# Three score steps in one row-tiled visit: a static order rebuilt on a refitted model

## The chip, the cores and the metric

The kernel runs on one core of a Trainium2 chip. The metric is the device time of one execution in microseconds. The kernel before takes 408.64 us in the median of 3 runs (407.82 to 408.83).

## The reference

Input is one sequence of 2048 tokens with 512 features in bf16. The same pair of blocks is applied twice, with the same weights.

```python
def _A_ref(x, wqkv, wo):              # H = 32 heads of 16, window W = 256
    qkv = (x @ wqkv).reshape(B, S, 3, H, Dh).transpose(2, 0, 3, 1, 4)
    scores = jnp.einsum("bhqd,bhkd->bhqk", q, k) * (Dh ** -0.5)
    mask = (idx[:, None] - idx[None, :] >= 0) & (idx[:, None] - idx[None, :] < W)
    p = _softmax(jnp.where(mask[None, None], scores, -1e9))
    o = jnp.einsum("bhqk,bhkd->bhqd", p, v)
    return o.transpose(0, 2, 1, 3).reshape(B, S, D) @ wo
def _B_ref(x, w_r, w_gate, w_up, w_down):
    r = x @ w_r
    ...                               # the ONE token with the largest r
    y = (_silu(x_sel @ w_gate) * (x_sel @ w_up)) @ w_down * _sigmoid(r_sel)
    return x + upd                    # y added to that token's row
x = x + _A_ref(_layernorm(x), A_wqkv, A_wo)
x = x + _B_ref(_layernorm(x), B_w_r, B_w_gate, B_w_up, B_w_down)
```

So each layer is attention over a sliding window of 256 keys for every token, and a gated MLP of width 1792 for a single token, which can be named only when all tokens of the layer have been through attention.

## The kernel before, in words

The 2048 tokens are cut into 16 tiles of 128 in each layer, 32 in all. For one tile the work runs like this (PE is TensorE, DVE VectorE, ACT ScalarE, POOL GpSimd, SP the queue of SyncE):

- *Layer norm:* statistics on DVE (L699, L700), the rest on POOL, and a transpose by DMA into XNT (L715).
- *Projections:* q and k with 16 matmuls each, V with 4 wide ones. DVE evacuates each: V at L768, q at L1050, k at L753. From k, four more DVE instructions (L756) write four copies, each masked to one of four groups of heads, so that one matmul can serve four heads. All three projections and the output projection take turns in one PSUM bank, number 7.
- *Scores:* nine steps in a steady tile (4 and 8 in the first two tiles of a layer). A step is a function `scores` on PE, 8 to 16 matmuls that use half the rows of the array each (64*128, "row-tiled"); it writes one pair of the six score banks, pairs taken in turn (`b0 = 2 * (n % 3)`). One ACT instruction (L1182) takes the exponential of the pair. POOL masks the windows' edges in four places of a tile (L1188).
- *PV:* 96 matmuls of 128x68 on the full array (L1212) collect values and row sums in bank 6, in two halves of 48. After each half DVE takes a reciprocal (L781) and normalises (L783).
- *Output:* the normalised tile is transposed by DMA into OT, the output projection follows (4 wide matmuls, L796), and DVE adds the residual (L800). Then come the router's dot product and the statistics for the next layer.

Between the layers the router's maximum is found, the MLP of the one token runs on PE (L875 to L970), and DVE adds the row (`upd`, L981); at the end the same again.

Nothing of this order is decided on the chip. While the program is built, a class `Sched` collects every operation with its engine, what it reads and writes, a duration in ns and a priority, and plays a list scheduler: the free engine takes, of the operations that are ready, the one with the smallest priority number. What comes out is one fixed instruction list for each engine, with semaphore waits where one needs another's result. So a duration or a priority changes only the order of the lists. Priorities are counted in tiles: `ln`, `prj`, `attend` and `fin` put a tile's layer norm, projections, attention and output at `(n - 2.4)`, `(n - 0.8)`, `n` and `(n + 1.3)` tile times.

`bind` ties steps together. Where PE changes between row-tiled and full-array matmuls, the array has to be emptied; steps that are tied run as one *visit* to the row-tiled mode. Before, each odd step is tied to the even one ahead of it:

```python
if n % 2:
    S.bind(self.tied, i)
self.tied = i
```

`cut` marks the place of the branch after the first MLP: operations that start in the model's time before `upd` ends plus 200 ns stand ahead of it in each engine's list, the others behind.

Of the kernel before, what the change touches and what calls it, by code (L numbers as in the profile page):

```python
# [57 lines left out]
class _Op:  # L58
    __slots__ = ("idx", "eng", "fn", "deps", "dur", "name", "is_dma", "prio", "signals", "count",
                 "dma_sem", "start", "end", "waits", "dma_extra", "soft", "tr", "keys", "layer", "glue")  # L60

    def __init__(self, idx, eng, fn, deps, dur, name, is_dma, prio):
# [19 lines left out]
        self.glue = None  # L82


class Sched:
    ENGS = ("pe", "act", "dve", "pool", "sp")

# [79 lines left out]
    def bind(self, i, j):  # L167
        a, b = self.ops[i], self.ops[j]
        a.glue = j
        for d in b.deps:  # L170
            if d != i:
                a.deps.add(d)
                if d in b.soft:
                    a.soft.add(d)
        b.deps.add(i)
        b.soft.add(i)

    def schedule(self):
        ops = self.ops
        n = len(ops)  # L180
# [4 lines left out]
        remaining = [len(op.deps) for op in ops]  # L185
# [31 lines left out]
        while done < n:  # L217
            best = None
            for e in self.ENGS:
# [1350 lines left out]
```

## Time and profile before

| | |
|---|---|
| median of 3 runs | 408.64 us (407.82 to 408.83) |
| profiled execution | 409.7 us |
| span of its instructions | 407.9 us |
| mean granted clock of PE | 0.946 of full |
| busy: PE, DVE, ACT, POOL | 347.8, 278.6, 266.3, 254.5 us |

Busy time counts an instruction from start to end; matmuls are pipelined, so a busy PE is not one at its peak. The span's share says which engine does much, not which one the end waits for; for that the chain of waits and the timeline of a single stretch are read.

### The profile page before, as it was taken

To read this page: it belongs to the slowest core of one execution; us is meant where nothing else is said; L and a number is where in the kernel's file an instruction comes from. 1 tells how busy PE (TensorE), PEld (TensorE's weight loads), DVE (VectorE), ACT (ScalarE), POOL (GpSimd) and SP (SyncE) were. 2 spreads that over 40 slices of the span, in tenths; PEclk is the share of its full clock that TensorE was granted. 3 is DMA by queue.
4 is the path that set the end of the run, shared out by engine and by line. 5 is a ranking of instruction groups with operands and counts; after the bars stand their busy time and mean duration, and the time that the engine had idled before them with its cause. 6 is when DMAs were issued, how large, how long until landed. Compare 5 with 4: busy or idle time off the path is not lost.

```text
span 407.9 us, 17608 instructions
## 1 busy us (share of the span) xinstructions
PE 347.8 (85%) x7740; PEld 277.1 (68%) x7793; DVE 278.6 (68%) x695; ACT 266.3 (65%) x284; POOL 254.5 (62%) x475
## 2 busy tenths in 40 slices
PE   6689698999999998986878699798889898986970
PEld 2477586877778787775767267677777787775560
DVE  5967876877777776675674388787777676673620
ACT  1078376787878787875764078687778787878000
POOL 5768866887878686766533069887566565556300
PEclk9779799999999999999999689999999999999965
DMA  8534434444435662433221013232422335221000
GB/s 267 170 73 55 100 116 81 128 131 100 117 76 107 78 118 65 102 71 81 57 41 40 3 44 84 55 69 55 75 57 63 70 68 69 56 56 27 14 18 5
DMA packets 72723, 31.23 MB, mean 77 GB/s; under 512 B 52672, under 2 KB 72000, under 8 KB 72640
## 3 DMA queue, kind: packets, MB, share of 16 engines
q1 hardware_dynamic: 70384, 27.81, 31.9%
q10 hardware_dynamic: 2256, 2.23, 1.7%
q8 instruction: 62, 1.02, 1.2%
q14 instruction: 21, 0.17, 0.2%
HBM read 14.29 MB, written 7.87 MB: 54 GB/s over the span
## 4 chain that ended last, share of the span: by engine, by line
PE 54%; DVE 24%; ACT 8%; DMA 5%; POOL 3%; issue 3%; SPq 1%; DVEq 0%; ACTq 0%; POOLq 0%
PE f_PS L1212 18%; PE f_PS L1172 10%; PE f_PS L739 10%; DVE f_KT L756 8%; ACT f_PT L1182 8%; PE f_PS L796 6%; DVE f_KTN L753 3%; DVE f_QT L1050 2%; DVE f_JUNK L813 2%; DMA f_OT<-f_ONORM 2%; PE f_PS L765 2%; PE f_PS L1233 2%; DVE f_xres L800 2%; DVE f_ST L811 2%; PE f_PS L933 2%
## 5 line engine op out<-in xcount | busy, mean ns | idle before, releaser
L1182 ACT ACTIVATE f_PT<-f_PS 128x1024 bf16<-128x1024 f32 x276 | 263.1, 1027 | 106.9 <-PE f_PS L1172 74.8
L1188 POOL TENSOR_TENSOR f_PT<-f_PT,f_TM 128x384 bf16<-128x384 bf16 x128 | 119.6, 935 | 72.8 <-ACT f_PT L1182 71.7
L1212 PE MATMUL f_PS<-f_VBD,f_PT 128*128 128x68 bf16 x2880 | 120.1, 198 | 7.4 <-DVE f_ONORM L783 2.6
L1212 PEld LDWEIGHTS f_PS<-f_VBD,f_PT 128*128 128x128 bf16 x2880 | 106.1, 99 | 25.1 <-issue 7.1
L1172 PE MATMUL f_PS<-f_QT,f_KT 64*128 64x128 bf16 (+3 forms) x2976 | 93.8, 204 | 7.1 <-DVE f_QT L1050 3.1
L1172 PEld LDWEIGHTS f_PS<-f_QT,f_KT 64*128 64x128 bf16 x2976 | 70.4, 94 | 28.3 <-ACT f_PT L1182 13.0
L739 PE MATMUL f_PS<-f_XNT,f_wqkv 128*128 128x128 bf16 x1024 | 70.5, 224 | 4.6 <-DVE f_KTN L753 1.6
L739 PEld LDWEIGHTS f_PS<-f_XNT,f_wqkv 128*128 128x128 bf16 x1024 | 60.1, 100 | 9.0 <-DVE f_KTN L753 1.8
L756 DVE TENSOR_SCALAR f_KT<-f_KTN,f_KM 128x512 bf16<-128x512 bf16 x128 | 58.5, 515 | 0.9
L796 PE MATMUL f_PS<-f_wo,f_OT 128*128 128x512 bf16 x98 | 27.9, 396 | 18.3 <-DVE f_RDA L781 9.5
L753 DVE CAST f_KTN<-f_PS 128x512 bf16<-128x512 f32 x32 | 22.1, 689 | 28.0 <-PE f_PS L739 27.9
L765 PE MATMUL f_PS<-f_wqkv,f_XNT 128*128 128x512 bf16 x108 | 29.7, 387 | 2.0 <-issue 0.9
L781 DVE RECIPROCAL f_RDA<-f_PS 128x16 f32<-128x16 f32 x64 | 16.1, 252 | 19.6 <-PE f_PS L1212 19.3
L783 DVE TENSOR_TENSOR f_ONORM<-f_PS,f_RDA 128x256 bf16<-128x256 f32 x64 | 26.5, 415 | 1.1
L768 DVE CAST f_VN<-f_PS 128x512 bf16<-128x512 f32 x32 | 22.0, 689 | 7.7 <-PE f_PS L765 7.5
L796 PEld LDWEIGHTS f_PS<-f_wo,f_OT 128*128 128x128 bf16 x128 | 10.4, 99 | 24.3 <-issue 13.7
L1170 PE MATMUL f_PS<-f_BM,f_II 64*128 64x64 bf16 (+1 forms) x256 | 24.8, 190 | 0.0
L813 DVE SCALAR_TENSOR_TENSOR f_JUNK<-f_xres,f_WR 128x512 bf16<-128x512 f32 x32 | 23.8, 743 | 0.0
L1050 DVE CAST f_QT<-f_PS 128x512 bf16<-128x512 f32 x32 | 21.8, 681 | 2.4 <-PE f_PS L739 2.4
L701 POOL TENSOR_SCALAR f_MV<-f_MV 128x1 f32<-128x1 f32 x32 | 6.1, 190 | 26.0 <-DVE f_MV L700 23.8
L811 DVE BATCH_NORM_STATS2 f_ST<-f_xres 128x6 f32<-128x512 f32 x32 | 21.5, 672 | 0.4
L800 DVE TENSOR_TENSOR f_xres<-f_PS,f_xin 128x512 f32<-128x512 f32 x16 | 11.1, 692 | 14.6 <-PE f_PS L796 14.5
(128 smaller groups left out, 306.8 us busy)
## 6 DMA issues: line engine op xcount, KB each, us to landing
f_vscr<-f_VN SPq DMA_DIRECT2D x32, 136.0 KB, 2.6
f_VBD<-f_vscr SPq DMA_DIRECT2D x128, 34.0 KB, 2.3
out_dram<-f_OUTB SPq DMA_DIRECT2D x16, 128.0 KB, 2.2
f_xin<-in_B_w_down_dram SPq DMA_DIRECT2D x14, 128.0 KB, 2.9
f_wg<-in_B_w_gate_dram SPq DMA_DIRECT2D x7, 256.0 KB, 3.7
f_wu<-in_B_w_up_dram SPq DMA_DIRECT2D x7, 256.0 KB, 3.5
f_wqkv<-in_A_wqkv_dram ACTq DMA_DIRECT2D x3, 512.0 KB, 5.6
f_xscr<-f_xres SPq DMA_DIRECT2D x5, 256.0 KB, 2.8
```

The lines of the kernel that those rows point to most:

```text
L739: r = e.matmul(self.bank(MB)[:, 128 * s:128 * s + 128], lhsT=self.wqkv[:, kc, off:off + 128], rhs=self.XNT[:, k2, kc, :], start=(kc == 0), ...
L753: S.add("dve", lambda e: e.tensor_copy(out=self.KTN[:, k2], in_=self.bank(MB)[:, 0:512].rearrange("p (s t) -> p s t", s=4)), reads=[], wri ...
L756: S.add("dve", lambda e, hh=hh: e.tensor_scalar(out=self.KT[:, k4, :, :, hh, :].rearrange("p s b k -> p (s b) k"), in0=self.KTN[:, k2].rea ...
L765: return e.matmul(self.bank(MB)[:, 0:512], lhsT=self.XNT[:, k2, kc, :], rhs=self.wqkv[:, kc, 1024:1536], start=(kc == 0), stop=(kc == 3))
L796: return e.matmul(self.bank(MB)[:, 0:512], lhsT=self.OT[:, ko, kc, :], rhs=self.wo[:, kc, :], start=(kc == 0), stop=(kc == 3))
L811: S.add(D, lambda e: e.bn_stats(out=self.ST6[:, 1, km, :], in_=x), reads=[xk], writes=["st6m%d" % km], dur=700, name="bnst2")
L813: S.add(D, lambda e: e.scalar_tensor_tensor(out=self.JUNK[:], in0=x, scalar=1.0, in1=self.WR16[:], op0=ALU.mult, op1=ALU.mult, accum_out=s ...
L1050: self.S.add("dve", lambda e: e.tensor_copy(out=self.QT[:, k2], in_=self.bank(MB)[:, 0:512].rearrange("p (s t) -> p s t", s=4)), reads=[], ...
L1172: r = e.matmul(o, lhsT=self.KT[p, (b // 4) % 4, s, b % 4].rearrange("p h k -> p (h k)"), rhs=self.QT[p, k2, s, q:q + w], start=(i == 0), s ...
L1182: S.add("act", lambda e: e.activation(out=view, in_=self.PS[:, b0:b0 + 2, 0:128 * nu].rearrange("p h (u c) -> p h u c", u=nu), func=ACTF.E ...
L1188: S.add("pool", lambda e: e.tensor_tensor(out=w, in0=w, in1=self.TM[:].unsqueeze(1).broadcast_to([128, k, 2, 32]), op=ALU.mult), reads=["t ...
L1212: r = e.matmul(self.bank(BK_PV)[:, c0:c0 + 68], lhsT=self.PT[:, w1:w1 + 128], rhs=self.VBD[:, (b // 4) % 4, b % 4].rearrange("p h (g c) -> ...
```

## The change

The scheduler's model of the chip is replaced by another, and three steps make a visit in place of two. The arithmetic on the chip and the instructions stay; only their order on each engine, and so the waits, move.

- `bind` takes a list of steps. The first one (the head) need not wait in the model until all inputs of the later ones are there: each such input may come as late as the steps ahead of it last, plus a slack `P_LEAD` of 224.787 ns.
- `VISIT = 3`: three steps, all six score banks, make one visit.
- The model gets an overlap per engine (`OVER`), a delay for each pair of engines (`HOP`) in place of one for all, and a price for each mode change (`TO_ROWS`, `TO_FULL`). Durations are new: a step 183 to 266 ns by its number of matmuls, an exponential 1022 (before 930), a masked copy 470 (before 270).
- New priorities: `P_LN` -2.934 for -2.4, `P_PRJ` -1.175 for -0.8, `P_FIN` 1.042 for 1.3, and others for q, k, V, the steps, PV and the MLP.
- The cut lies 2500 ns behind `upd`, before 200.

```diff
+    OVER = {"pe": 0.0, "act": 105.0, "dve": 82.0, "pool": 20.0, "sp": -35.0}
+    HOP = {"act": {"pool": 77.0, "pe": 51.0, "dve": 32.0, "sp": 28.0, "act": 34.0},
...
+    TO_ROWS = 122.0
+    TO_FULL = 184.0
...
-    def bind(self, i, j):
-        a, b = self.ops[i], self.ops[j]
-        a.glue = j
-        for d in b.deps:
-            if d != i:
-                a.deps.add(d)
-                if d in b.soft:
-                    a.soft.add(d)
-        b.deps.add(i)
-        b.soft.add(i)
+    def bind(self, ids, slack=0.0):
+        ops = self.ops
+        head = ops[ids[0]]
+        off = head.dur + slack
+        lead = {}
+        for i, j in zip(ids, ids[1:]):
+            ops[i].glue = j
+            for d in ops[j].deps:
+                if d not in ids and d not in head.deps:
+                    lead[d] = min(lead.get(d, 1e9), off)
+            ops[j].deps.add(i)
+            ops[j].soft.add(i)
+            off += ops[j].dur
+        head.lead = tuple(lead.items())
...
+            if e == "pe" and op.rows != rows:
+                rows = op.rows
+                st += self.TO_ROWS if rows else self.TO_FULL
...
+    P_STEP = 1.453
+    P_NORM = -0.028
+    P_LEAD = 224.787
+    VISIT = 3
+    P_LN = -2.934
+    P_PRJ = -1.175
+    P_FIN = 1.042
...
-              dur=sum(max(27, w[4] / 2.4 + 3) for w in work) + 98, name="scores")
-        if n % 2:
-            S.bind(self.tied, i)
-        self.tied = i
+              dur={8: 183, 10: 213, 14: 211, 16: 266}.get(2 * len(work), 20 * 2 * len(work)), name="scores")
+        S.ops[i].rows = True
+        if n % self.VISIT == 0:
+            self.tied = []
+        self.tied.append(i)
+        if n % self.VISIT == self.VISIT - 1:
+            S.bind(self.tied, self.P_LEAD)
...
-            fs.cut(upd_op.end + 200.0)
+            fs.cut(upd_op.end + 2500.0)
```

Three places show what the scheduler makes of this. The line numbers of the kernel after are larger: scores L1231 (before L1172), a small matmul that adds a mask inside a step L1229 (L1170), q and k projections L781 (L739), PV L1274 (L1212), output projection L843 (L796), masked copies L802 (L756), q evacuation L1109 (L1050).

PE in a steady tile, before (in layer 2, from one visit to the next but one):

```order
L1172 MATMUL f_PS<-f_QT,f_KT 128x128 x10
L1212 MATMUL f_PS<-f_VBD,f_PT 128x68 x14
L739 MATMUL f_PS<-f_XNT,f_wqkv 128x128 x16
L1212 MATMUL f_PS<-f_VBD,f_PT 128x68 x12
L1172 MATMUL f_PS<-f_QT,f_KT 128x32 x2
L1172 MATMUL f_PS<-f_QT,f_KT 128x96 x4
L1172 MATMUL f_PS<-f_QT,f_KT 128x32 x2
L1172 MATMUL f_PS<-f_QT,f_KT 128x64 x4
L1172 MATMUL f_PS<-f_QT,f_KT 128x128 x6
L1170 MATMUL f_PS<-f_BM,f_II 128x64 x2
L1172 MATMUL f_PS<-f_QT,f_KT 128x128 x4
L796 MATMUL f_PS<-f_wo,f_OT 128x512 x4
```

And after, in a steady tile of layer 1:

```order
L781 MATMUL f_PS<-f_XNT,f_wqkv 128x128 x16
L1274 MATMUL f_PS<-f_VBD,f_PT 128x68 x22
L1231 MATMUL f_PS<-f_QT,f_KT 128x128 x8
L1231 MATMUL f_PS<-f_QT,f_KT 128x32 x2
L1231 MATMUL f_PS<-f_QT,f_KT 128x96 x4
L1231 MATMUL f_PS<-f_QT,f_KT 128x32 x2
L1231 MATMUL f_PS<-f_QT,f_KT 128x64 x4
L1231 MATMUL f_PS<-f_QT,f_KT 128x128 x6
L1229 MATMUL f_PS<-f_BM,f_II 128x64 x2
L1231 MATMUL f_PS<-f_QT,f_KT 128x128 x4
L781 MATMUL f_PS<-f_XNT,f_wqkv 128x128 x16
```

A visit before holds 22 to 24 small matmuls, of which the first rows here end one and the last rows show one that is followed by the output projection; after, it holds 32 to 38. In a whole steady tile before (mean of two tiles, which alternate) stand 4.5 visits, after 3: one of 38 matmuls ahead of the output projection, one of 34 behind the V projection, one of 32 between the k and the q projection, as here. Ahead of that last one stand 22 PV matmuls, behind the q projection 26, and then the next tile's visit of 38.

DVE around the evacuation of k and q, before (layer 2):

```order
L753 CAST f_KTN<-f_PS 128x512
L756 TENSOR_SCALAR f_KT<-f_KTN,f_KM 128x16x32 x4
L1050 CAST f_QT<-f_PS 128x512
L781 RECIPROCAL f_RDA<-f_PS 128x16
L783 TENSOR_TENSOR f_ONORM<-f_PS,f_RDA 128x256
L700 BN_AGGR f_MV<-f_ST 128x2
```

And after:

```order
L799 CAST f_KTN<-f_PS 128x512
L802 TENSOR_SCALAR f_KT<-f_KTN,f_KM 128x16x32 x4
L742 BN_AGGR f_MV<-f_ST 128x2
L741 BN_STATS f_ST<-f_xin 128x6
L1109 CAST f_QT<-f_PS 128x512
L828 RECIPROCAL f_RDA<-f_PS 128x16
L830 TENSOR_TENSOR f_ONORM<-f_PS,f_RDA 128x256
```

After, an aggregate and the statistics of a later tile's layer norm stand between the masked copies (L802) and the q evacuation (L1109); before, in this place, nothing does. The row behind it is a reciprocal in both.

PE from the last up projection of the first MLP to the branch, before:

```order
L1212 MATMUL f_PS<-f_VBD,f_PT 128x68 x22
L933 MATMUL f_PS<-f_XS,f_wu 128x1 x56
L739 MATMUL f_PS<-f_XNT,f_wqkv 128x128 x16
L970 MATMUL f_PS<-f_xin,f_HT 128x512 x14
L739 MATMUL f_PS<-f_XNT,f_wqkv 128x128 x16
L1479 TENSOR_LOAD flag
L1479 ISA x2
L1480 COMPARE_AND_BRANCH
L796 MATMUL f_PS<-f_wo,f_OT 128x512 x4
```

And after:

```order
L1274 MATMUL f_PS<-f_VBD,f_PT 128x68 x4
L980 MATMUL f_PS<-f_XS,f_wu 128x1 x28
L1274 MATMUL f_PS<-f_VBD,f_PT 128x68 x18
L812 MATMUL f_PS<-f_wqkv,f_XNT 128x512 x4
L1274 MATMUL f_PS<-f_VBD,f_PT 128x68 x30
L1017 MATMUL f_PS<-f_xin,f_HT 128x512 x14
L781 MATMUL f_PS<-f_XNT,f_wqkv 128x128 x32
L1541 TENSOR_LOAD flag
L1541 ISA x2
L1542 COMPARE_AND_BRANCH
L1231 MATMUL f_PS<-f_QT,f_KT 128x32 x2
```

L970 and L1017 are the down projection of the MLP, which waits for its hidden vector. Before, the k projection of the next layer's tile stands ahead of it, and q behind it; after, 48 PV matmuls and a V projection stand ahead, k and q behind. Behind the branch, the kernel before goes on with an output projection, the kernel after with the first visit of a tile.

## Rows read from the trace of the kernel before

**Rows 1.** The page's chain that ended last: share of the span by engine.

```profile
PE 54%; DVE 24%; ACT 8%; DMA 5%; POOL 3%; issue 3%; SPq 1%; DVEq 0%; ACTq 0%; POOLq 0%
```

**Rows 2.** The page's costliest groups: busy us, mean ns; idle before, releaser.

```profile
L1182 ACT ACTIVATE f_PT<-f_PS 128x1024 bf16<-128x1024 f32 x276 | 263.1, 1027 | 106.9 <-PE f_PS L1172 74.8
L1188 POOL TENSOR_TENSOR f_PT<-f_PT,f_TM 128x384 bf16<-128x384 bf16 x128 | 119.6, 935 | 72.8 <-ACT f_PT L1182 71.7
```

**Rows 3.** Timeline of PE in layer 1: start us, us, operation, count, idle before.

```profile
165.18 1.04 PE L765 MATMUL f_PS<-f_wqkv,f_XNT 128*128 128x512 bf16 x4
166.15 0.54 PE L1172 MATMUL f_PS<-f_QT,f_KT 64*128 64x32 bf16 x18
...
166.91 1.74 PE L1212 MATMUL f_PS<-f_VBD,f_PT 128*128 128x68 bf16 x48
168.58 0.54 PE L1172 MATMUL f_PS<-f_QT,f_KT 64*128 64x128 bf16 x18
168.95 0.19 PE L1170 MATMUL f_PS<-f_BM,f_II 64*128 64x64 bf16 x2
...
169.19 1.07 PE L739 MATMUL f_PS<-f_XNT,f_wqkv 128*128 128x128 bf16 x16
170.09 0.88 PE L1212 MATMUL f_PS<-f_VBD,f_PT 128*128 128x68 bf16 x22
170.90 0.40 PE L1172 MATMUL f_PS<-f_QT,f_KT 64*128 64x128 bf16 x8
```

**Rows 4.** Timeline of PE: four starts of the output projection.

```profile
80.43 0.81 PE L796 MATMUL f_PS<-f_wo,f_OT 128*128 128x512 bf16 x3
...
174.03 0.81 PE L796 MATMUL f_PS<-f_wo,f_OT 128*128 128x512 bf16 x3 [0.16 <-issue]
...
245.33 0.81 PE L796 MATMUL f_PS<-f_wo,f_OT 128*128 128x512 bf16 x3 [0.16 <-issue]
...
364.37 0.81 PE L796 MATMUL f_PS<-f_wo,f_OT 128*128 128x512 bf16 x3 [1.19 <-DVE f_RDA L781]
```

**Rows 5.** Timeline of ACT in layer 1, beside rows 3.

```profile
164.93 3.77 ACT L1182 ACTIVATE f_PT<-f_PS 128x1024 bf16<-128x1024 f32 x4 [1.03 <-PE f_PS L1172]
169.05 1.94 ACT L1182 ACTIVATE f_PT<-f_PS 128x1024 bf16<-128x1024 f32 x2 [0.35 <-PE f_PS L1172]
```

**Rows 6.** Timeline of PE in layer 2: a k projection.

```profile
306.17 1.06 PE L739 MATMUL f_PS<-f_XNT,f_wqkv 128*128 128x128 bf16 x16
```

**Rows 7.** Timeline of DVE: masked copies of K, and those around them.

```profile
13.63 5.20 DVE L756 TENSOR_SCALAR f_KT<-f_KTN,f_KM 128x512 bf16<-128x512 bf16 x4
...
118.30 1.16 DVE L756 TENSOR_SCALAR f_KT<-f_KTN,f_KM 128x512 bf16<-128x512 bf16 x4
...
159.54 1.59 DVE L756 TENSOR_SCALAR f_KT<-f_KTN,f_KM 128x512 bf16<-128x512 bf16 x4
...
297.45 1.89 DVE L756 TENSOR_SCALAR f_KT<-f_KTN,f_KM 128x512 bf16<-128x512 bf16 x4
...
307.26 0.69 DVE L753 CAST f_KTN<-f_PS 128x512 bf16<-128x512 f32 x1 [1.56 <-PE f_PS L739]
307.99 2.15 DVE L756 TENSOR_SCALAR f_KT<-f_KTN,f_KM 128x512 bf16<-128x512 bf16 x4
310.05 0.68 DVE L1050 CAST f_QT<-f_PS 128x512 bf16<-128x512 f32 x1
```

**Rows 8.** Groups of DVE instructions by line: busy us, mean ns; idle before.

```profile
L699 DVE BATCH_NORM_STATS2 f_ST<-f_xres 128x6 f32<-128x512 f32 x16 | 10.8, 682 | 0.4 <-DVE f_QT L1050 0.2
```

**Rows 9.** The attention output's tile: its transposing DMA, issue to landing.

```profile
DMA to landing us min/median/max: 2.4/2.5/4.6
```

**Rows 10.** Two stretches (busy of five engines, PEclk, DMA), and PE's timeline there.

```profile
46.00:52.60 6.60, 5.24 (x75) 4.05 (x76) 4.63 (x12) 1.94 (x2) 4.77 (x13) 0.50 0.44 128
223.70:230.00 6.30, 5.22 (x13) 1.90 (x14) 1.69 (x5) 0.00 (x0) 0.00 (x0) 0.50 0.04 6
...
224.78 5.71 PE L970 MATMUL f_PS<-f_xin,f_HT 128*128 128x512 bf16 x13 [1.26 <-DVE f_KT L756]
```

More of the change, by code (lines that the diff above doesn't have):

```diff
@@ L59 @@
     __slots__ = ("idx", "eng", "fn", "deps", "dur", "name", "is_dma", "prio", "signals", "count",
-                 "dma_sem", "start", "end", "waits", "dma_extra", "soft", "tr", "keys", "layer", "glue")
+                 "dma_sem", "start", "end", "waits", "dma_extra", "soft", "tr", "keys", "layer", "glue", "rows", "lead")
     def __init__(self, idx, eng, fn, deps, dur, name, is_dma, prio):
@@ L184, in schedule @@
                 users[d].append(op.idx)
-        remaining = [len(op.deps) for op in ops]
+        remaining = [len(op.deps) + len(op.lead) for op in ops]
+        early = {}
+        for op in ops:
+            for d, off in op.lead:
+                early.setdefault(d, []).append((op.idx, off))
         after = {}
@@ L212, in schedule @@
         pin = {e: None for e in self.ENGS}
+        rows = False
         def blocked(i):
@@ L321, in schedule @@
                 remaining[u] -= 1
-                rt = st if u in late else op.end + (0.0 if i in ops[u].soft else self.sem_latency)
+                if u in late:
+                    rt = st
+                elif i in ops[u].soft:
+                    rt = busy_end
+                else:
+                    rt = op.end + self.HOP[e][ops[u].eng]
                 if rt > ready_time[u]:
@@ L334, in schedule @@
                         _heappush(fut[ue], (rt, ops[u].prio, u))
+            for u, off in early.get(i, ()):
+                remaining[u] -= 1
+                ready_time[u] = max(ready_time[u], op.end + self.HOP[e]["pe"] - off)
+                if remaining[u] == 0:
+                    rt = ready_time[u]
+                    if rt <= t_eng["pe"]:
+                        _heappush(now["pe"], (ops[u].prio, u))
+                    else:
+                        _heappush(fut["pe"], (rt, ops[u].prio, u))
         self.order = order
@@ L1026 @@
     RING = 10
+    P_Q = 0.041
+    P_K = -0.027
+    P_V = -0.444
+    P_STEP = 1.453
[5 more added lines that the diff above has]
+    P_FIN = 1.042
+    P_MG = 0.121
+    P_PV = 0.878
     warm0 = 21
@@ L1215, in f @@
             return r
-        S.add("pe", f, reads=[ptk] + pz + ["vb%d_%d" % (x, hh) for x in pslots for hh in range(4)], writes=["bank%d" % BK_PV], dur=63 * len(part), name="pv")
+        S.add("pe", f, reads=[ptk] + pz + ["vb%d_%d" % (x, hh) for x in pslots for hh in range(4)], writes=["bank%d" % BK_PV], dur=62.6 * len(part), name="pv")
     def vstore(self, m):
@@ L1238, in attend @@
         steps = self.plan(m)
-        d = 0.8e6 / len(steps)
+        d = self.P_STEP * 1e6 / len(steps)
         self.pvhalf = None
```

38 lines of the change are left out of this document (27 added, 11 removed).

## The prediction

> **What bounds the kernel now.** I read the chain of waits first. TensorE (PE) holds 54% of the chain that ended last, VectorE (DVE) 24%, ScalarE (ACT) 8% [rows 1]. So neither the exponentials nor the masks set the pace, although each fills much of its engine: ACT waited 106.9 us in front of its exponentials, 74.8 of them for score matmuls [rows 2].
>
> Then the timeline of PE in one steady stretch, where it does not wait [rows 3]. It gives the price of each piece at full clock, from start to start. 48 PV matmuls up to the next visit take 168.58 - 166.91 = 1.67 us and 22 take 170.90 - 170.09 = 0.81, so one costs 0.86 / 26 = 33 ns and the entry into a row-tiled visit 0.08. The reader is to see this small entry: the mode change is cheap. A visit of two steps lasts 169.19 - 168.58 = 0.61, its first 18 matmuls 168.95 - 168.58 = 0.37, so 20.5 ns each. A projection of 16 matmuls takes 170.09 - 169.19 = 0.90, one of four wide ones 166.15 - 165.18 - 0.08 = 0.89.
>
> A tile holds 96 PV matmuls (3.18 us), k and q projections (1.80), V and output projections (1.78) and 4.5 visits of 0.61 + 0.08 (3.11): 9.87 us. The starts of the output projection say how long a tile really takes: (174.03 - 80.43) / 9 = 10.40 us in layer 1 and (364.37 - 245.33) / 11 = 10.82 in layer 2 [rows 4]. So 0.5 us of each tile in layer 1 and 0.95 in layer 2 is PE waiting. The last of those rows shows on whom: 1.19 us that ended with a DVE reciprocal, which stands behind the masked copies of K and the q evacuation in DVE's queue.
>
> **The change part by part.** Nothing is computed otherwise, so every instruction keeps its row's duration; only order and waits change.
>
> *Fewer visits.* Steady tiles get 3 visits of three steps in place of 4.5 of two. A third step adds some 12 matmuls: 12 x 20.5 = 0.24 us, so a visit is 0.85 and with its entry 0.93, and three are 2.79. That saves 0.32 us of PE a tile. The bounds: a third step of 8 matmuls is 0.16, one of 14 is 0.29, which gives 0.56 and 0.17. Without waits a tile would last 9.87 - 0.32 = 9.55 (9.54 piece by piece below).
>
> *The new wait.* In the new order a visit fills all six score banks, so the third step of a visit needs the last exponential of the visit before. Exponentials come at (3.77 - 1.02) / 3 = 0.92 us, the first of them 169.05 - 168.58 = 0.47 after the visit's start [rows 3, 5] (1.02 from the mean in [rows 2]). From the second visit of a tile to the third step of the next tile's first visit lie six of them: 0.47 + 6 x 0.92 = 5.99, then that step (0.24), the output projection, 40 PV, V and the entry (0.89 + 1.32 + 0.97): 9.4 us until the second visit starts again. That is under 9.55, so the six banks alone do not set the pace.
>
> *What is late next: k to q.* In the new order DVE does, for one tile: K evacuation, four masked copies, an aggregate and the statistics of a later tile, then q evacuation; and the tile's first visit on PE waits for q. Behind that visit stand the output projection, PV and V on PE, and behind these the residual and the V store on DVE and SyncE's queue. The chain from rows: k projection's start to K evacuation 307.26 - 306.17 = 1.09, evacuation to copies 307.99 - 307.26 = 0.73 [rows 6, 7]; the copies; statistics 0.68 [rows 8] and 0.07 of the aggregate not hidden; q evacuation 0.68 less the 0.09 by which DVE's rows overlap (307.99 + 2.15 - 310.05), so 0.60; 0.05 to PE. The copies took 1.16, 1.59, 1.89 and 2.15 us in four tiles [rows 7], depending on what GpSimd does meanwhile. Their mean 1.70 is the value I take; 1.16 and 2.15 are kept as ends. Sum: 1.09 + 0.73 + 1.70 + 0.75 + 0.60 + 0.05 = 4.92.
>
> PE has beside it k (0.90), 22 PV with entry (0.81), a visit (0.85), q (0.90), 26 PV with entry (0.94): 4.40. So PE waits 0.52 in front of each first visit. The rest of the tile, from that visit to the next k projection: 0.85 + 0.89 + 1.32 + 0.89 + 0.08 + 0.85 + 0.26 = 5.14. The tile: 4.92 + 5.14 = 10.06 us.
>
> A price that the trace cannot show is how the copies meet GpSimd in the new order. The bounds are 1.16 (then PE's own 9.54 holds) and the 5.20 of the kernel's start [rows 7], which would make 8.42 + 5.14 = 13.56; it is far from the rows of the steady tiles, so I keep 2.15 as the working end. By the Trainium skill (SBUF — State Buffer, Who interferes with whom), a DVE tensor_scalar in a two-port mode and a GpSimd instruction exclude each other for a whole instruction, "the other **fully blocks**". By that alone each of four copies could wait for one mask, and the copies would last 1.16 + 4 x 0.91 = 4.8 (an estimate from that page with the mask's mean [rows 2]); the steady rows of this trace stop at 2.15, so they bear the rule out in direction, not in that size.
>
> *Output projection one tile later.* It now reads the transposed tile two visits' worth later. The DMA lands in 2.4 to 4.6 us, median 2.5 [rows 9]; from the normalisation to its use the new order leaves about half a tile, so I count nothing, and up to 0.5 us in a rare tile.
>
> *Layers.* Layer 1: 12 such tiles x (10.40 - 10.06) = 4.1. Layer 2: 11 x (10.82 - 10.06) = 8.4.
>
> *Middle.* The 14 down matmuls ran 5.71 us at a granted clock of 0.50, the 1.2 GHz level, after PE had waited 1.26 for DVE [rows 10]. In the new order 48 PV matmuls and a V projection stand directly ahead of them (2.5 us of work), in place of a lone projection. I expect the 2.4 GHz level and half the time, -2.8. Behind the branch the first visit now waits for K evacuation, copies, statistics and q evacuation in a row (0.73 + 1.16 + 0.75 + 0.60 = 3.24), where before copies were done ahead of it: +1.1 as I take it, 0 to +2. Net -1.7.
>
> *Early hole.* Between 46 and 52.6 us the clock was 0.50 and PE idle for 1.36 us [rows 10]. The new order fills this ramp with larger visits. At full clock that stretch is 3.3 us shorter; with the waits in front of it up to 6 are to be had, or none if the hole only moves. I take -3.
>
> *Tail.* The final router and MLP are unchanged: 0.
>
> Sum: -4.1 - 8.4 - 1.7 - 3 = -17.2. The profiled execution took 409.7, so 392.5 by its own measure; it lies 1.06 above the median of 408.64, and against that I say 391.
>
> **The rivals.**
> (a) *PE alone sets the pace.* Copies take 1.16 everywhere, as in the shortest of the rows; the wait vanishes and the tile is 9.54. Then 12 x 0.86 + 11 x 1.28 = 24.4, with 4.7 more: -29.1, thus 379.6. For it: ACT's loop allows 9.4. Against: GpSimd's masks now come in threes behind three exponentials, so the copies rarely find it idle.
> (b) *Contention eats it.* Copies at 2.15 make the tile 10.51: layer 1 loses 1.3, layer 2 gains 3.4, with 4.7 this is 402, and 405 if the early hole stays. For it: the two rows of layer 2, 1.89 and 2.15 [rows 7].
> (c) *Slower: DVE takes over.* One mechanism: the wait in front of the first visit, once per tile. It decides when the copies pass 2.44 us: then 12 x 10.40 + 11 x 10.82 + 4.7 = 248.5 = 23 x 10.80, nothing gained. At 2.65 the tile is 11.0 and the kernel 4.5 us slower, 413. If that wait also brings the 1.2 GHz level, as between 46 and 52.6 us, the first visit and what follows for some us cost twice, and 420 is passed. Against: waits of 1.19 in layer 2 [rows 4] ended in projections at full speed (0.81).
> (d) *The order changes on paper, no matter on the chip:* waits fall where PE waited already. Then the 0.32 of PE is lost in an equal wait: 408, within 0.3%.
>
> **How the numbers follow.** Forecast (copies between 1.4 and 2.0, 384 to 400): 0.60. (a) 0.15. (b) 0.13, of which a small part ends within 0.3%. (c) 0.09. (d) 0.03. About 0.3% is what a measurement here can tell from no change. Faster 0.87, same 0.04, slower 0.09. The range 380 to 404 leaves out half of (a), the end of (b), (c) and (d), 0.19 in all.
>
> **What would show it.** Right: output projections 10.0 to 10.2 apart in both layers; an idle time of about half a us in front of each tile's first visit, ended by the q evacuation; 92 visits; copies at 1.7; down matmuls near 2.9. A third step that waits for an exponential by over 0.3 us in each visit would say that my ACT loop is too short; tiles of 9.6 speak for (a); idle time of over 1 us ended by the q evacuation for (c). The forecast is wrong if the tile's period does not fall in layer 1, or if the early stretch at 1.2 GHz grows.

## The result: 389.22 us, 4.5% less, and the profile after

The kernel after takes 389.22 us in the median of 4 runs (387.40 to 391.38), the kernel before 408.23 beside it (4 runs, 404.37 to 408.83). The ratio is 0.9555, with a 95% interval of 0.9475 to 0.9636. Ratios, here and below, are taken over the fast executions of the two kernels alone, so they can differ from the quotient of the medians beside them. The profiled execution took 390.14 us with a span of 388.4, at a mean clock of 0.954.

The chain that ended last and the two costliest groups of ACT and GpSimd (POOL) on the page after answer to [rows 1, 2]:

```profile
PE 65%; DVE 15%; POOL 9%; DMA 3%; issue 3%; ACT 2%; DVEq 0%; ACTq 0%; POOLq 0%
...
L1244 ACT ACTIVATE f_PT<-f_PS 128x1024 bf16<-128x1024 f32 x276 | 261.6, 1025 | 85.0 <-PE f_PS L1231 60.9
L1250 POOL TENSOR_TENSOR f_PT<-f_PT,f_TM 128x384 bf16<-128x384 bf16 x128 | 127.7, 999 | 53.3 <-ACT f_PT L1244 51.7
```

PE's share of the chain went up from 54 to 65%, DVE's down from 24 to 15%, and POOL's up from 3 to 9%: less of the end is set by waits for DVE. ACT idles 85.0 us in front of its exponentials, before 106.9. GpSimd's masks became longer, 999 ns for 935.

PE's timeline of one steady tile after (layer 1; to be read like [rows 3]), from one output projection to the next:

```profile
147.46 1.04 PE L843 MATMUL f_PS<-f_wo,f_OT 128*128 128x512 bf16 x4
148.33 1.47 PE L1274 MATMUL f_PS<-f_VBD,f_PT 128*128 128x68 bf16 x40
149.63 1.03 PE L812 MATMUL f_PS<-f_wqkv,f_XNT 128*128 128x512 bf16 x4
150.59 0.29 PE L1231 MATMUL f_PS<-f_QT,f_KT 64*128 64x128 bf16 x4
...
151.46 0.43 PE L1274 MATMUL f_PS<-f_VBD,f_PT 128*128 128x68 bf16 x8
151.73 1.06 PE L781 MATMUL f_PS<-f_XNT,f_wqkv 128*128 128x128 bf16 x16
152.94 0.88 PE L1274 MATMUL f_PS<-f_VBD,f_PT 128*128 128x68 bf16 x22 [0.16 <-issue]
153.75 0.76 PE L1231 MATMUL f_PS<-f_QT,f_KT 64*128 64x128 bf16 x26
...
154.59 1.07 PE L781 MATMUL f_PS<-f_XNT,f_wqkv 128*128 128x128 bf16 x16
155.49 1.01 PE L1274 MATMUL f_PS<-f_VBD,f_PT 128*128 128x68 bf16 x26
156.53 0.54 PE L1231 MATMUL f_PS<-f_QT,f_KT 64*128 64x32 bf16 x18
...
157.46 1.04 PE L843 MATMUL f_PS<-f_wo,f_OT 128*128 128x512 bf16 x4
```

Taken from start to start, the reader can price each piece: output projection 0.87, 40 PV 1.30, V 0.96, a visit 0.87, 8 PV 0.27, k projection 152.94 - 151.73 = 1.21, 22 PV 0.81, a visit 0.84, q projection 0.90, 26 PV 156.53 - 155.49 = 1.04, the tile's first visit 0.93: 10.00 us (most steady tiles take 9.95 to 9.96, with a k projection of 1.17). Two pieces are longer than the same work in [rows 3]: the k projection (0.90 there) by 0.31, the 26 PV (0.94 by the prices there) by 0.10. There PE waits, although the view marks only part of it.

DVE's timeline beside it says for what:

```profile
151.93 0.26 DVE L828 RECIPROCAL f_RDA<-f_PS 128x16 f32<-128x16 f32 x1 [0.41 <-PE f_PS L1274]
152.22 0.42 DVE L830 TENSOR_TENSOR f_ONORM<-f_PS,f_RDA 128x256 bf16<-128x256 f32 x1
152.82 0.69 DVE L799 CAST f_KTN<-f_PS 128x512 bf16<-128x512 f32 x1 [0.18 <-PE f_PS L781]
153.55 1.16 DVE L802 TENSOR_SCALAR f_KT<-f_KTN,f_KM 128x512 bf16<-128x512 bf16 x4
155.69 0.69 DVE L1109 CAST f_QT<-f_PS 128x512 bf16<-128x512 f32 x1 [0.98 <-PE f_PS L781]
```

The reciprocal starts 0.20 after PE has gone on from the 8 PV to the k projection (151.73), the normalisation ends at 152.64, and PE's next PV matmul, which writes the same bank, starts 0.30 behind it. That way takes 1.2 us and the k projection beside it lasts only 0.9. The masked copies took 1.16 and the q evacuation stood idle for 0.98 us until the q projection was there; PE's first visit then starts 0.15 behind the evacuation (156.53 against 155.69 + 0.69). No aggregate and no statistics stand here between the copies and the q evacuation. The order shown above the prediction, with both in this place, is that of seven tiles of layer 1; in layer 2 no tile has statistics there.

A third wait lies inside the tile's first visit. Its third step needs the banks of the third exponential from the visit before; the view of PE begins with that step:

```profile
156.02 1.03 ACT L1244 ACTIVATE f_PT<-f_PS 128x1024 bf16<-128x1024 f32 x1
...
157.10 0.36 PE L1231 MATMUL f_PS<-f_QT,f_KT 64*128 64x128 bf16 x10
```

The exponential ends at 157.05 and the step starts 0.05 later, and so in 17 other tiles; the visit takes 0.93 us, and 0.86 in tiles where this step doesn't wait. So even if q had been there 0.10 sooner, the exponential would have held the visit's third step to the same moment.

Where the 19.5 us of span went, by the starts of the output projections on PE (the new order puts this projection later within its tile, so the edges shift by parts of a tile):

| stretch | before | after | difference |
|---|---|---|---|
| start to the 3rd of layer 1 | 61.28 | 56.10 | -5.2 |
| 3rd to 16th (13 periods) | 135.16 | 131.05 | -4.1 |
| 16th to the 2nd of layer 2 (middle) | 37.81 | 39.59 | +1.8 |
| 2nd to 14th of layer 2 (12 periods) | 130.12 | 120.82 | -9.3 |
| 14th to the end of the span | 43.53 | 40.84 | -2.7 |

Two cautions. Most starts before are those of the second of four matmuls, the first having no record, so these edges are late by up to 0.2 us. And the trace before is of an execution of 409.7 us, longer than the four timed ones. In the trace of the old order with freed heads (further down; 405.4 us) the first two rows are 58.30 and 132.87, the next two 37.76 and 130.56. So some 3 us of the first row and 2 of the second may be that one execution's and not the change's. Its clock between 46 and 52.6 us differs, too; the first line is of that run, the second of the kernel after, and [rows 10] has 0.50 there:

```profile
46.00:52.60 6.60, 5.81 (x145) 4.63 (x148) 6.40 (x18) 4.42 (x5) 5.67 (x15) 1.00 0.44 128
...
46.00:52.60 6.60, 5.22 (x138) 4.28 (x136) 4.78 (x13) 3.96 (x6) 5.96 (x13) 1.00 0.43 132
```

Four of these starts after, which answer to [rows 4]:

```profile
107.65 1.04 PE L843 MATMUL f_PS<-f_wo,f_OT 128*128 128x512 bf16 x4
...
167.41 1.04 PE L843 MATMUL f_PS<-f_wo,f_OT 128*128 128x512 bf16 x4
```

```profile
267.90 1.04 PE L843 MATMUL f_PS<-f_wo,f_OT 128*128 128x512 bf16 x4
...
347.56 1.04 PE L843 MATMUL f_PS<-f_wo,f_OT 128*128 128x512 bf16 x4
```

(167.41 - 107.65) / 6 = 9.96 us and (347.56 - 267.90) / 8 = 9.96: the same tile in both layers, where before the means differed by 0.42.

The middle after, PE's timeline and the granted clock (column before the last two) in three stretches; it answers to [rows 10]:

```profile
216.47 3.19 PE L1017 MATMUL f_PS<-f_xin,f_HT 128*128 128x512 bf16 x14
...
222.92 1.58 PE L781 MATMUL f_PS<-f_XNT,f_wqkv 128*128 128x128 bf16 x16 [1.34 <-DVE f_KTN L799]
225.29 0.83 PE L1231 MATMUL f_PS<-f_QT,f_KT 64*128 64x32 bf16 x18 [0.79 <-DVE f_QT L1109]
```

```profile
212.00:216.00 4.00, 4.00 (x69) 2.90 (x67) 1.37 (x4) 0.00 (x0) 0.00 (x0) 0.63 0.02 4
222.00:226.00 4.00, 2.30 (x38) 2.04 (x40) 3.96 (x11) 0.06 (x1) 0.51 (x2) 0.66 0.03 8
226.00:229.00 3.00, 3.00 (x37) 1.53 (x34) 1.69 (x5) 2.79 (x3) 2.72 (x6) 0.50 0.00 0
```

The down matmuls took 3.19 us instead of 5.71. But PE ran at 0.63 ahead of them, and behind the branch PE waited 1.34 us for the K evacuation and 0.79 for the q evacuation; from 222 to 229 us the clock was 0.66, then 0.50, the 1.2 GHz level. The first visit there took 1.45 us (0.93 in a steady tile), the output projection behind it 1.82 (0.87).

### The profile page after: what moved, and what is told of

Read it like the earlier page. It is cut to its first block, busy times and chain, and to the rows that moved or that the text cites. A ratio compares the mean times of both kernels' runs of the same rounds, so it can differ in the third digit from the quotient of the medians.

```text
span 388.4 us, 17651 instructions
## 1 busy us (share of the span) xinstructions
PE 346.4 (89%) x7793; PEld 277.5 (71%) x7793; DVE 268.0 (69%) x695; ACT 264.9 (68%) x284; POOL 266.3 (69%) x475
## 3 DMA queue, kind: packets, MB, share of 16 engines
q8 instruction: 62, 1.02, 1.2%
## 4 chain that ended last, share of the span: by engine, by line
PE 65%; DVE 15%; POOL 9%; DMA 3%; issue 3%; ACT 2%; DVEq 0%; ACTq 0%; POOLq 0%
PE f_PS L1274 20%; PE f_PS L1231 15%; PE f_PS L781 11%; PE f_PS L843 7%; PE f_PS L812 6%; DVE f_KT L802 3%; DMA f_OT<-f_ONORM 2%; PE f_PS L1295 2%; POOL f_PT L1250 2%; DVE f_ST L741 2%; ACT f_PT L1244 1%; DVE f_VN L815 1%; POOL f_xres L867 1%; POOL f_XN L749 1%; DVE f_QT L1109 1%
## 5 line engine op out<-in xcount | busy, mean ns | idle before, releaser
L1250 POOL TENSOR_TENSOR f_PT<-f_PT,f_TM 128x384 bf16<-128x384 bf16 x128 | 127.7, 999 | 53.3 <-ACT f_PT L1244 51.7
L1274 PE MATMUL f_PS<-f_VBD,f_PT 128*128 128x68 bf16 x2880 | 115.5, 198 | 7.6 <-DVE f_ONORM L830 4.6
L1274 PEld LDWEIGHTS f_PS<-f_VBD,f_PT 128*128 128x128 bf16 x2880 | 105.2, 98 | 22.5 <-issue 12.1
L1231 PE MATMUL f_PS<-f_QT,f_KT 64*128 64x128 bf16 (+3 forms) x2976 | 89.3, 205 | 9.8 <-DVE f_QT L1109 5.8
L1231 PEld LDWEIGHTS f_PS<-f_QT,f_KT 64*128 64x128 bf16 x2976 | 72.7, 95 | 29.3 <-issue 14.7
L781 PE MATMUL f_PS<-f_XNT,f_wqkv 128*128 128x128 bf16 x1024 | 70.7, 225 | 5.6 <-DVE f_GWR L928 2.1
L781 PEld LDWEIGHTS f_PS<-f_XNT,f_wqkv 128*128 128x128 bf16 x1024 | 60.5, 100 | 10.2 <-DVE f_KTN L799 2.6
L802 DVE TENSOR_SCALAR f_KT<-f_KTN,f_KM 128x512 bf16<-128x512 bf16 x128 | 47.8, 434 | 0.9
L843 PE MATMUL f_PS<-f_wo,f_OT 128*128 128x512 bf16 x128 | 34.8, 396 | 2.5 <-DMA f_OT<-f_ONORM 1.8
L812 PE MATMUL f_PS<-f_wqkv,f_XNT 128*128 128x512 bf16 x128 | 34.0, 389 | 0.5 <-DVE f_MV L742 0.5
L1109 DVE CAST f_QT<-f_PS 128x512 bf16<-128x512 f32 x32 | 21.9, 685 | 10.7 <-PE f_PS L781 10.3
L1229 PE MATMUL f_PS<-f_BM,f_II 64*128 64x64 bf16 (+1 forms) x256 | 25.4, 192 | 0.0
L847 DVE TENSOR_TENSOR f_xres<-f_PS,f_xres 128x512 f32<-128x512 f32 x16 | 11.0, 691 | 16.8 <-PE f_PS L843 16.8
L860 DVE SCALAR_TENSOR_TENSOR f_JUNK<-f_xres,f_WR 128x512 bf16<-128x512 f32 x32 | 21.8, 681 | 0.1
```

The source lines that it names most:

```text
L781: r = e.matmul(self.bank(MB)[:, 128 * s:128 * s + 128], lhsT=self.wqkv[:, kc, off:off + 128], rhs=self.XNT[:, k2, kc, :], start=(kc == 0), ...
L802: S.add("dve", lambda e, hh=hh: e.tensor_scalar(out=self.KT[:, k4, :, :, hh, :].rearrange("p s b k -> p (s b) k"), in0=self.KTN[:, k2].rea ...
L812: return e.matmul(self.bank(MB)[:, 0:512], lhsT=self.XNT[:, k2, kc, :], rhs=self.wqkv[:, kc, 1024:1536], start=(kc == 0), stop=(kc == 3))
L843: return e.matmul(self.bank(MB)[:, 0:512], lhsT=self.OT[:, ko, kc, :], rhs=self.wo[:, kc, :], start=(kc == 0), stop=(kc == 3))
L1109: self.S.add("dve", lambda e: e.tensor_copy(out=self.QT[:, k2], in_=self.bank(MB)[:, 0:512].rearrange("p (s t) -> p s t", s=4)), reads=[], ...
L1229: r = e.matmul(o, lhsT=self.II[p, :], rhs=self.BM[p, q:q + w], start=False, stop=True, skip_group_check=True)
```

## The experiments

Each ran with the kernel before beside it on its chip, and ratios are to that one.

**Two steps in a visit.**

```diff
-    VISIT = 3
+    VISIT = 2
```

> The kernel after with two steps in a visit (VISIT = 2), everything else as it is. Theory A, the three-step visits carry the gain: two-step visits give back 0.32 us of PE per tile and, as the order is no longer one of a single tile, some of the waits; tiles of 10.2 to 10.4 us, so 397 to 404 us. Theory B, the refitted model and priorities carry it and the visit length is worth little: 388 to 393 us.

402.91 us, before 405.48; ratio 0.9886 (0.9794 to 0.9979). Theory A holds as far as it goes: without the third step three quarters of the gain are gone (by the interval, from half to nearly all). The scheduler finds another order for it, no longer one of a single tile, and the largest group of PE's waits is for the K evacuation, 8.1 us in 11 waits, in the kernel before 1.6. So the run changes more than the visits' length.

**Three steps on the old model.**

```diff
-        if n % 2:
-            S.bind(self.tied, i)
-        self.tied = i
+        if n % 3:
+            S.bind(self.tied[-1], i)
+            for x in self.tied[:-1]:
+                for d in S.ops[i].deps:
+                    if d not in self.tied:
+                        S.ops[x].deps.add(d)
...
+        else:
+            self.tied = []
+        self.tied.append(i)
```

> The kernel before with its old model and priorities, and three steps tied instead of two. Theory A: the visits alone bring most of the 19 us, 389 to 394. Theory B: without the new priorities the waits on DVE stay (0.5 to 0.95 us a tile), so only the 0.32 us of PE a tile are gained: 27 tiles x 0.32 = 9 us, 398 to 402.

420.26 us, before 405.48; ratio 1.0425 (1.0327 to 1.0524). Both theories missed: three steps on the old model are slower than two. The largest group of waits of PE in this run (in total, times, longest):

```profile
PE f_PS L1172 <- ACT f_PT L1190: 10.8, 20, 1.4
```

PE waits for exponentials in front of scores (L1172) for 10.8 us; in the kernel before it was 1.8. That pointed to the wait at the head of a visit, which the old `bind` hands from the later steps to the first, and the new one does not.

**The same order, with the wait at the head.**

```diff
     S.schedule()
+    for ids in visits:
+        a = S.ops[ids[0]]
+        for i in ids[1:]:
+            for d in S.ops[i].deps:
+                if d not in ids:
+                    a.deps.add(d)
...
```

> The kernel after with the same order on every engine, but the first step of each visit waits on the chip for what its second and third step need too (as pairs did in the kernel before); in the kernel after each step waits for its own banks only. Theory: with six banks in one visit this costs: the last visit of a tile can start only when the exponentials of the one before are all done (3.3 us after its start, now 3.16) and the next tile's first one likewise (now 2.78): 0.6 to 0.8 us a tile, 27 tiles, 405 to 410, and PE's wait for exponentials is what grows. Rival: PE is late enough anyway that the wait is hidden: 389 to 391.

406.50 us, before 405.55; ratio 1.0014 (0.9974 to 1.0054): the theory holds. Every engine has the instructions of the kernel after in the same order, and the whole gain is gone. PE's waits for exponentials in front of scores are 26.1 us in 58 waits, after 0.4 in 2. A steady tile on PE:

```profile
143.93 0.81 PE L843 MATMUL f_PS<-f_wo,f_OT 128*128 128x512 bf16 x3 [0.16 <-issue]
...
150.22 0.76 PE L1232 MATMUL f_PS<-f_QT,f_KT 64*128 64x128 bf16 x26 [0.20 <-ACT f_PT L1246]
...
153.57 0.54 PE L1232 MATMUL f_PS<-f_QT,f_KT 64*128 64x32 bf16 x18 [0.60 <-ACT f_PT L1246]
...
154.65 0.81 PE L843 MATMUL f_PS<-f_wo,f_OT 128*128 128x512 bf16 x3 [0.16 <-issue]
```

The tile takes 154.65 - 143.93 = 10.72 us, 0.76 more than after, and the two new waits are 0.20 and 0.60, both ended by an exponential, in front of the visit between k and q and in front of the tile's first one. So in this kernel a visit over all six banks is worth having only if each of its steps waits for its own pair.

**The old order, without the wait at the head.**

```diff
+            self.heads.append((self.tied, set(S.ops[self.tied].deps)))
             S.bind(self.tied, i)
...
     S.schedule()
+    for i, own in heads:
+        S.ops[i].deps = own
```

> The kernel before, its order on every engine unchanged, but the first step of each pair waits on the chip for its own banks only, as in the kernel after. Theory H, the wait at the head of a visit was what the change took away: 6 to 14 us less, 391 to 400. Theory O, with pairs one of the three bank pairs is always free, PE waited for exponentials only 1.8 us in 4 waits, so this wait costs little in the old order: 402 to 406 (before on this chip 405.5), and the freer head is worth its 17 us only in visits that fill all six banks.

405.29 us, before 406.66; ratio 1.0013 (0.9968 to 1.0058): no difference. Theory O holds: with pairs, one of three bank pairs is free anyway, and PE's waits for exponentials in front of scores only fell from 1.8 us to 0.8. So the freed head is needed for the gain, and by itself it brings none. Three steps on the old model with each step waiting for its own banks was not tried, so what the refitted model adds beside those two stays open.

**One more reciprocal.**

```diff
+            if half == 1 and self.PRE == "f_":
+                e.reciprocal(out=self.XR[:, self.xr % 64, :], in_=acc[:, :, 16])
+                self.xr += 1
+            return e.reciprocal(out=rd, in_=acc[:, :, 16])
```

> The kernel after with one more reciprocal (128x16, about 0.26 to 0.29 us) on DVE ahead of the normalisation of each tile's second PV half, its result unused. Reading of the trace after: PE waits there, since the k projection (0.90 us) covers less than the way from the last PV of the half over reciprocal and normalisation back to the next PV matmul (1.17 us). Then the whole instruction is on the path in each of some 28 tiles: +7 to +8 us, 396 to 398, tiles of 10.22. The chain of the prediction (k projection, masked copies, q evacuation) has no room for this instruction: then 389 to 391, tiles of 9.95.

390.81 us, before 405.48; ratio 0.9638 (0.9567 to 0.9709). The time is what the second theory says, but within the noise of the kernel after, so it decides nothing; the trace does:

```profile
152.86 0.26 DVE L833 RECIPROCAL f_XR<-f_PS 128x16 f32<-128x16 f32 x1 [0.41 <-PE f_PS L1282]
153.04 0.20 DVE L835 RECIPROCAL f_RDA<-f_PS 128x16 f32<-128x16 f32 x1
```

```profile
152.66 1.06 PE L784 MATMUL f_PS<-f_XNT,f_wqkv 128*128 128x128 bf16 x16
153.94 0.88 PE L1282 MATMUL f_PS<-f_VBD,f_PT 128*128 128x68 bf16 x22 [0.23 <-POOL f_xres L875]
```

The second reciprocal starts 0.18 after the first and lasts 0.20, so the way grew by 0.1 and not by the 0.26 to 0.29 that I had expected: k projection to PV is 1.28 here, 1.17 to 1.21 after. (The view names a GpSimd operation as what ended the 0.23; PV reads nothing of what that writes, and the normalisation ended 0.25 ahead of PV.) The tile is 10.06 (158.68 to 168.74 between output projections), against 9.95 to 9.96. All of the added 0.1 is in the tile: this wait is on its path. The chain of the prediction would have left the tile as it was.

**The accumulator copied out.**

```diff
+            cp = self.ACC[:, ko]
+            acc = cp.rearrange("p (h c) -> p h c", c=17)
...
+            self.early.append((i, j, ko, lambda e: e.tensor_copy(out=cp, in_=self.bank(BK_PV)[:, 0:272])))
...
+        if op.name == "pv":
+            for d in [d for d in op.deps if d in src]:
+                op.deps.discard(d)
+                op.deps.add(src[d])
```

> The kernel after, but DVE copies the second PV half's accumulator (128x272) to SBUF, about 0.45 us, and takes reciprocal and normalisation from the copy; the next tile's PV waits for the copy alone. Same order on every engine. Reading of the trace after: the way back to PE shrinks from 1.17 to about 0.9 us, which the k projection covers; tiles of 9.68 to 9.75, 28 x 0.2 to 0.27 = 6 to 7.5 us less: 382 to 384. Rival: another wait (q evacuation ahead of the first visit, six score banks) stands right behind and takes the gain: 387 to 390. The added 0.45 us of DVE could also delay the masked copies, but the q evacuation waits 0.95 us for PE.

388.94 us, before 405.48; ratio 0.9601 (0.9551 to 0.9651), no gain in time: the rival holds. But in five steady tiles PE takes 9.68 and in a sixth 9.71, with no wait behind the k projection (the rows are of the sixth):

```profile
154.37 1.06 PE L784 MATMUL f_PS<-f_XNT,f_wqkv 128*128 128x128 bf16 x16
155.31 0.88 PE L1283 MATMUL f_PS<-f_VBD,f_PT 128*128 128x68 bf16 x22
```

0.94 instead of 1.21. That confirms the cause from its other side. Elsewhere it was given back. The DVE timeline of the longest tile (11.68 us), and PE's first visit that waits for it:

```profile
115.90 2.56 DVE L805 TENSOR_SCALAR f_KT<-f_KTN,f_KM 128x512 bf16<-128x512 bf16 x4
...
118.58 0.69 DVE L744 BATCH_NORM_STATS2 f_ST<-f_xres 128x6 f32<-128x512 f32 x1
119.19 0.67 DVE L1118 CAST f_QT<-f_PS 128x512 bf16<-128x512 f32 x1
```

```profile
120.01 0.54 PE L1240 MATMUL f_PS<-f_QT,f_KT 64*128 64x32 bf16 x18 [1.65 <-DVE f_QT L1118]
```

This is the chain of the prediction in full: slow copies, aggregate, statistics, and PE waits 1.65 us for q.

**Two more masked copies.**

```diff
+                    if hh >= 2 and self.PRE == "f_":
+                        e.tensor_scalar(out=self.XK[:, k2, :, :, hh - 2, :].rearrange("p s b k -> p (s b) k"), in0=src,
+                                        scalar1=self.KM[:, hh:hh + 1], scalar2=None, op0=ALU.mult)
```

> The kernel after with two more masked copies (128x512, 0.29 us each, to an unused tile) on DVE between the K evacuation and the q evacuation of each tile. The chain of the prediction (k projection, copies, statistics, q evacuation, first visit) has them on the path: +0.58 us a tile, 28 tiles, +16 us: 403 to 406. Reading of the trace after: the q evacuation waits 0.95 us for the q projection in steady tiles, so they are hidden there, and only the tiles whose copies take 2.0 us or carry statistics behind them lose: +1 to +4 us, 390 to 394.

402.16 us, before 405.55; ratio 0.9906 (0.9863 to 0.9950): 13 us more than after, near what the chain of the prediction said, and far from my reading of the trace after. The tiles say why. Eight tiles, four in a row in each layer, stay at 9.95: there no statistics stand behind the copies. Where they do, the tile takes 10.17 to 11.17, three in a row 10.55:

```profile
131.56 0.69 DVE L743 BATCH_NORM_STATS2 f_ST<-f_xres 128x6 f32<-128x512 f32 x1
132.18 0.67 DVE L1116 CAST f_QT<-f_PS 128x512 bf16<-128x512 f32 x1
```

```profile
133.00 0.54 PE L1238 MATMUL f_PS<-f_QT,f_KT 64*128 64x32 bf16 x18 [0.70 <-DVE f_QT L1116]
```

So the idle 0.95 us ahead of the q evacuation is a cushion that one of the two, two copies or the statistics, uses up; both together are late. Five tiles late in layer 2 take 10.25 to 10.38; there the copies of the kernel after, too, take 2.0. But 8 us of the loss lie outside the steady tiles: ahead of the third projection (60.15 for 56.10) and in the middle (43.9 us from the 16th to the 18th, for 39.6). So that the total comes near the chain's 0.58 for each tile is in part chance.

**The q evacuation ahead of the statistics.**

```diff
+        if ops[q[n]].name == "evq":
+            k = n
+            while ops[q[k - 1]].name in ("bnst", "aggr") and q[k - 1] not in ops[q[k]].deps:
+                q[k - 1], q[k] = q[k], q[k - 1]
+                k -= 1
```

> The kernel after, with the q evacuation moved ahead of the aggregate and the statistics that stand between it and the masked copies on DVE (a dozen tiles; PE, ACT, POOL and SP as they are). If these statistics are what makes PE wait for the q evacuation (5.8 us in 8 waits): 2 to 4 us less, 385 to 387. If those waits come from slow copies or from the q projection: 389 to 390.

388.26 us, before 405.55; ratio 0.9570 (0.9503 to 0.9637). All tiles of layer 1 between the 4th and the 14th projection now take 9.94 to 9.95, where after three took 10.3 to 11.0. So in those tiles the chain of the prediction did bind. The time is 1 us less, under the 2 to 4 expected, which the spread of these runs doesn't resolve.

**Both together,** measured twice, the second time with the kernel after beside it.

> The accumulator copy of the run before together with the q evacuation ahead of the statistics. In that run half of the tiles took 9.68 us, the others 9.9 to 11.7, the longest with 2.56 us of copies and 0.85 of aggregate and statistics ahead of the q evacuation. If the statistics made them long: 383 to 386. If the copies beside GpSimd and the late transposing DMA of the output did: 387 to 389.

> The kernel with the accumulator copy and the q evacuation ahead of the statistics, beside the kernel after on one chip: it beats it by 1.5 to 3 us, since about half of its steady tiles take 9.68 in place of 9.95 (14 x 0.27 = 3.8) and three or four in layer 2 take longer. If not: the tiles that run into GpSimd's masks take back all of it.

> The kernel after once more, as the measure for the two runs beside it on the same chip: 387 to 391, steady tiles of 9.95 us.

387.14 us (384.58 to 388.58) in the first, ratio 0.9543 (0.9489 to 0.9598). In the second 387.10 us (384.83 to 388.02) against 389.18 of the kernel after (386.30 to 391.54) on one chip, 6 runs each, with ratios to the kernel before of 0.9548 (0.9486 to 0.9611) and 0.9588 (0.9510 to 0.9666). So it is 2 us better in the medians, with ranges that overlap; that it beats the kernel after is likely, not shown. Most tiles of layer 1 are 9.68, but some of layer 2 take 9.9 to 10.7, with copies of 2.0 to 2.3 beside GpSimd: of the first two theories the second holds. The half of the tiles at 9.68 from which these expectations start was too many: in the copying-out run it was the six named there.

**The cut.**

```diff
-            fs.cut(upd_op.end + 2500.0)
+            fs.cut(upd_op.end + 200.0)
```

> The kernel after with the cut 200 ns behind the update of the token's row, as before, in place of 2500: a q projection on PE, four masked copies and a tile's statistics on DVE move behind the branch. If the wider cut shortens the restart behind the branch: 1 to 2 us more, 390 to 392. If PE waits there for the K and q evacuation anyway: within 0.5 us of the kernel after.

388.66 us against 389.18 of the kernel after beside it: no difference that these runs resolve, and nothing speaks for the wider cut as a part of the gain. The middle (16th projection to the 2nd of layer 2) takes 38.04 us in this trace, against 39.59 and, in a second trace of the kernel after, 41.50. Here the clock was 1.00 in the 4 us ahead of the down matmuls, where the first trace after has 0.63 and the other runs with this order have 0.50 to 0.65. With one trace of this cut, that the cut made the difference is not shown.

## Why the prediction came out, point by point

*The sum held, 391 for 389.2, in part by luck.* By the table the layers gave -13.4 for -12.5, the early hole -5.2 for -3, the tail -2.7 for 0 and the middle +1.8 for -1.7: the middle's miss offset part of the others. Within a tile, the wait that I had priced was not the one that came.

*Fewer visits:* right. The three visits took 0.93, 0.87 and 0.84; with the entries counted as there that is 2.88 us, said were 2.79, and 0.07 of it is the wait for an exponential.

*The new wait:* the loop over the six banks, 9.4 us, counts six exponentials without a pause. But the fourth starts 0.28 us late, since the third visit stands behind the wait for the normalisation, and the third step of the next first visit then waits for the last of them. So this way binds lightly, with 0.07 us beyond the wait for q, far under the 0.3 that I had named as a sign. And I took it for granted that each step waits for its own banks. The run with the wait at the head shows that without this, a few lines of `bind`, nothing of the gain is left: with it a tile is 10.72. It should have been a rival, with its price.

*k to q:* the failed step. I expected a wait of 0.52 in front of a tile's first visit, made by copies of 1.70 and 0.75 for the aggregate and the statistics in every tile. The copies took 1.1 to 1.3 in 21 of 32 tiles, and both of the others stand in this place in seven tiles only. With 1.16 and without the 0.75 my chain is 3.63 us, under PE's 4.40 beside it: the first visit waits 0.10, and the q evacuation waits for PE. What I left out is the way from the last PV of a tile over reciprocal and normalisation back to PE: of it 0.3 stands uncovered behind the k projection. This 0.3, the 0.10 and the 0.07, on PE's own 9.54, come near the 0.52, and so the tile came out right (10.06 against 9.96): luck in the size, with another mechanism. The copying-out run takes the 0.3 away and the tile falls to 9.68; the run with one more reciprocal lengthens it. The forecast chain is not wrong but second: it binds in three of the seven tiles of layer 1 that have the statistics (10.3 to 11.0 us), and two copies more or a slow GpSimd bring it forward.

*Output projection:* counted at nothing, rightly; PE's waits for its transposing DMA are 1.8 us in 2 waits, before 2.7 in 3.

*Rivals:* PE alone (9.54) was out by the waits that I overlooked. Contention (b) is there in single tiles, with copies of 2.0, which the cushion hides in the last tiles of layer 2. (c) comes to its edge in one tile of 10.98 us, with 1.0 us of waiting for q, and decides nothing in all. My 4.8 us for four blocked copies used 0.91 for a mask where [rows 2] has 0.935, which makes it 4.9; neither comes.

*Layers:* -4.1 and -9.3, for -4.1 and -8.4. A period went from 10.40 to 10.08 in layer 1 and from 10.84 to 10.07 in layer 2; the table counts one period more in each layer than I did. In the other trace of the old order a period of layer 1 is 10.22, so the -4.1 is less certain than the -9.3.

*Middle:* wrong in sign, by the edges of the table +1.8 for -1.7. The down matmuls came out near the forecast (3.19, said were 2.9). The restart was mis-sized: I said +1.1 behind the branch and left the clock out, which fell to 0.50 there. *Early hole:* -5.2 up to the 3rd projection, for -3; the stretch from 38 to 60 us now runs at a clock of 1.00. But with the old order and freed heads it does so too, and 3.0 of the 5.2 are there already; that the fuller ramp raised the clock is not shown. *Tail:* -2.7 for 0; I had looked only at its unchanged instructions, but layer 2's last tiles stand in it.

## What to carry to other kernels

When a change both reorders work and changes what an instruction waits for, run the new order with the old waits and the old order with the new waits: here neither alone was worth anything. A larger group of work that fills every buffer was worth it here only with each member waiting for its own buffer. And when pricing a loop, follow every way that leaves an engine and comes back to it (here PE, DVE, PE around one accumulator bank): a short one with little beside it can bind ahead of the long one.

## What the runs showed of the hardware

Four masked copies on DVE took 1.14 us or 2.03 in tiles whose order is the same. They differ in what GpSimd was doing. DVE and POOL in two tiles of the kernel after; the last DVE line is one of the second tile's four copies by itself:

```profile
303.89 1.14 DVE L802 TENSOR_SCALAR f_KT<-f_KTN,f_KM 128x512 bf16<-128x512 bf16 x4
...
323.80 2.03 DVE L802 TENSOR_SCALAR f_KT<-f_KTN,f_KM 128x512 bf16<-128x512 bf16 x4
...
324.29 1.02 DVE L802 TENSOR_SCALAR f_KT<-f_KTN,f_KM 128x512 bf16<-128x512 bf16 x1
```

```profile
304.24 1.26 POOL L882 TENSOR_SCALAR f_OUTB<-f_xres 128x512 bf16<-128x512 f32 x1 [0.18 <-POOL f_xres L873]
...
323.46 0.76 POOL L882 TENSOR_SCALAR f_OUTB<-f_xres 128x512 bf16<-128x512 f32 x1 [0.18 <-POOL f_xres L873]
324.25 0.91 POOL L1250 TENSOR_TENSOR f_PT<-f_PT,f_TM 128x384 bf16<-128x384 bf16 x1
```

In the first tile the copies had begun when GpSimd's 128x512 operation came, and that one took 1.26 us for its usual 0.76; in the second the operation was under way, a mask came right behind, and the copies took 2.03. The Trainium skill (SBUF — State Buffer, Who interferes with whom) says of a DVE instruction in a two-port mode and a GpSimd instruction that whoever issues first holds the shared pair of ports for the whole instruction and that the other blocks. These rows agree, instruction by instruction: one copy took 1.02 us and ended 0.15 behind the mask, while each of the two behind it took 0.34. The 4.8 us for the four copies that the prediction worked out from this, and set aside, doesn't come: only the copies that meet a GpSimd instruction pay, and the loss was 0.9 us for the group.

A normalisation on DVE took 0.39 to 0.43 us whenever it read the accumulator from PSUM; from the copy in SBUF, in the run with the accumulator copied out, it took 0.39 to 0.89, five of 32 over 0.6.
